# Splitting the last inverse-transform factor by even and odd frequency, on a quarter of the matrix engine each

## The chip, the cores and the metric

The kernel runs on one core of one Trainium2 chip. A core has a matrix engine (TensorE: PE in the profile, with its weight loads shown apart as PEld), a vector engine (DVE), a scalar engine (ACT), a general engine (POOL) and a queue engine (SP), which here only starts transfers (DMAs). The metric is the device time of the program in microseconds (us). Before the change the median of three runs is 2586.32 us (2583.95 to 2587.9).

## The reference

Two steps follow each other. The first is a filter in the frequency domain along the sequence; the second is a two-layer network with the ELU function between the layers. All is float32.

```python
# x: (8, 3008, 256); filt_r, filt_i: (1505, 256)
X = np.fft.rfft(x, axis=1)
y = np.fft.irfft(X * (filt_r + 1j * filt_i)[None], n=3008, axis=1)
# w_in: (256, 2048); w_out: (2048, 256)
h = y.reshape(24064, 256) @ w_in
out = np.where(h > 0, h, np.exp(np.minimum(h, 0)) - 1) @ w_out
```

## The kernel before, in words

**The transform.** The sequence of 3008 tokens is written as 47 x 64, so a token is 47·n2 + n1 with n2 from 0 to 63, and each direction of the transform takes two factors of matrix products with tables. Tokens n1 and 47 − n1 are handled as a pair i (24 pairs in all), because their tables are mirror images. The stages for one of the 8 batches b are: `x_unit` and `a_unit` (the first forward factor), `z_write` and `z_read` through memory, `b_unit` (the second forward factor), the products with the filter (`re_mult` to `im_sums`), `bi_unit` (the first inverse factor), `y_write`, and then, for each of six groups m of four pairs, `tn_read`, `y_read`, `n_unit` and `n_sums`. This last factor is what the diff touches.

`n_unit` sums over 128 rows, which are 32 frequencies k2 times four parts p (cosine and sine, of the pair's two sides). For each pair and each half dh of the 256 channels it multiplies a 128 x 128 tile of `t` (rows against channels) with a 128 x 128 tile of the table `tn` (rows against tokens: 64 values of n2 for n1, 64 for 47 − n1). That is eight matrix products a unit, into two PSUM banks, and ACT copies each bank to SBUF (`y0`, `y1`). The float32 product runs as two passes, so the profile shows 16 weight loads and 16 matmuls a unit.

**The network.** The two layers are computed with Strassen's scheme in Winograd's form: seven products in the place of eight, and sums ahead of them and behind them. Its blocks are the two channel halves and two token halves. `n_sums` makes the four sums of the input blocks on DVE (function `combine`: each a difference of two 128 x 256 tiles; 128 x 224 for m = 0, which has seven token sets in place of eight). `up_steps` makes the seven products of the first layer for a quarter q of the 2048 hidden columns, and the ELU: `keep` copies on ACT, `add` on DVE, `elu_exp` (two ACT instructions) and `elu_max` (one DVE instruction). `down_steps` makes the seven products of the second layer for the quarter before.

**The order.** It is written out by hand. One quad is one (b, m, q): seven U steps of this quarter and seven D steps of the one before, four matmul records each. A batch has 24 quads (`PER`). The transform's work is hung into the quads by a table, `at(quad, place, function)`: place 2 is behind the third step of the quad, place 3 behind the fifth, place 0 in the middle (behind seven or eight steps), place 1 behind the quad's last step and sums. Every engine runs its instructions in this order, so what is put at a place stands in line, on each engine that it uses, between the steps around it. With t the first quad of the batch before, the six units of `n_unit` stand at quads t+23, 25, 29, 32, 36, 40 and the network uses unit m from quad t+24+4m on. Their transfers are issued on SP's queue two quads earlier. The sums stand with the unit for m < 3 and one quad later, at place 1, for m > 2. A stage before the change that already uses parts of the matrix engine: `a_unit` has 64 x 64 tiles in groups of four (two row halves, two column halves), 256 columns wide; `b_unit` and `bi_unit` have sixteen tiles of 24 x 32.

The first batch has its own path (`a_first`, `t_first`, `b_first`, `bi_first`), since nothing else can run by then; weights are also prepared there on DVE and ACT, up to the fourth quad. `n_unit(0, 0)` and `n_sums(0, 0)` are called right ahead of the first quad.

In `up_steps` one DVE instruction will matter: step 7 puts its product into a bank "d", `add("b22", ...)` reads that bank, and step 4 then adds its own product into the same bank, so PE must not begin step 4 before that add has read it.

Of the kernel before, what the change touches and what calls it, by code (L numbers as in the profile page):

```python
# [26 lines left out]
P = 128  # L27
# [14 lines left out]
def _make_tables():  # L42
# [75 lines left out]
    gf = np.zeros_like(gb)  # L118
    for o in (0, 64):
        gf[o:o + 48] = gb[o:o + 48].reshape(2, H, 2, 64).swapaxes(0, 1).reshape(48, 2, 64)  # L120
    tn = np.ascontiguousarray(tn.reshape(4, K2, H, P).swapaxes(0, 1)).reshape(P, H, P)
    once = np.stack([np.eye(P), gf.reshape(P, P)], 1)
    return [t.astype(np.float32) for t in (ta, tn, np.stack([gb, gr, gi], 1), tf, once, pairs)]

# [7 lines left out]
def kernel(  # L132
# [60 lines left out]
    def bank(name, shape=(P, 2, D)):  # L193
        i = banks.pop(0)
        return i, psM.tile(list(shape), FP32, tag="m%d" % i, name=name)
# [271 lines left out]
                              t[32 * p:32 * p + 24])  # L467

    def tn_read(b, m):
        w = tns[b, m] = tnp.tile([P, 4, P], FP32, tag="tn", name="tn")  # L470
        nc.sync.dma_start(w, tn_d[:, 4 * m:4 * m + 4, :])

    def y_read(b, m, *parts):
        t = t4s[b, m] = t4p.tile([P, 4, D], FP32, tag="t4", name="t4")
        for k in parts or (slice(0, K2),):
            r = slice(4 * k.start, 4 * k.stop)
            nc.sync.dma_start(t[r], yds[b].rearrange("k (p i) d -> (k p) i d", p=4)[r, 4 * m:4 * m + 4, :])

    def half(m):

# [1 line left out]

    def n_unit(b, m):
        t, w, h = t4s.pop((b, m)), tns.pop((b, m)), half(m)
        rows = []
        for dh in range(2):
            y = yp.tile([P, 512], FP32, tag="y%d" % dh, name="y%d" % dh)
            k, ps = bank("psn", (P, 512))
            for q, i in enumerate(order(m)):
                nc.tensor.matmul(ps[:, ts(q, P)], t[:, i - 4 * m, ds(dh * P, P)], w[:, i - 4 * m, :],  # L490
                                 start=True, stop=True)
            nc.scalar.activation(out=y[:, 0:2 * h], in_=ps[:, 0:2 * h], func=AXT.Copy)
            banks.append(k)
            rows += [y[:, 0:h], y[:, h:2 * h]]
        s = yp.tile([P, 3, 256], FP32, tag="ys", name="ys")
        ys[b, m] = rows + [s[:, i, 0:h] for i in range(3)]

    def n_sums(b, m):
        ys[b, m] = combine(*ys[b, m])

    COMBO = {1: 0, 2: 2, 3: 6, 4: 3, 5: 4, 6: 5, 7: 1}

    def combine(b11, b12, b21, b22, t1, t2, t4):

        nc.vector.tensor_tensor(out=t1, in0=b12, in1=b11, op=ALU.subtract)
        nc.vector.tensor_tensor(out=b12, in0=b22, in1=b12, op=ALU.subtract)
        nc.vector.tensor_tensor(out=t2, in0=b22, in1=t1, op=ALU.subtract)
        nc.vector.tensor_tensor(out=t4, in0=b21, in1=t2, op=ALU.subtract)
        return {1: b11, 2: b21, 3: b22, 4: t4, 5: t1, 6: t2, 7: b12}  # L520

    G_TAGS = (("g1", ("b11", "b12")), ("g2", ("b21", "b22")), ("g3", ("t1", "t2")), ("g4", ("t4",)))
    UPS = (1, 2, 6, 5, 7, 3, 4)
# [2 lines left out]
    def up_steps(b, m, q):  # L526

        h = half(m)
        y = ys[b, m]
        g = {}  # L530
        for tag, names in G_TAGS:
            t = gp.tile([P, len(names), 2, 256], FP32, tag=tag, name=tag)
            g.update({n: t[:, i, :, 0:h] for i, n in enumerate(names)})
        held = {}

        def mm(n, key, start):
            if start:
                held[key] = bank("ph" + key)
            ps = held[key][1]
            for a in range(2):  # L540
                nc.tensor.matmul(ps[:, a, 0:h], w_in[q][:, COMBO[n], a, :], y[n],  # L541
                                 start=start and a == 0, stop=True, skip_group_check=True)
            return ps[:, :, 0:h]

        def done(key):
            banks.append(held.pop(key)[0])

        def add(o, i0, i1):
            nc.vector.tensor_tensor(out=g[o], in0=i0, in1=i1, op=ALU.add)  # L549

        def keep(o, i0):
            nc.scalar.activation(out=g[o], in_=i0, func=AXT.Copy)  # L552

        es = {}

        def elu_exp(n, src):
            e = es[n] = ep.tile([P, 2, 256], FP32, tag="e", name="e")[:, :, 0:h]
            nc.scalar.activation(out=e, in_=src, func=AXT.Relu, scale=-1.0)  # L558
            nc.scalar.activation(out=e, in_=e, func=AXT.Exp, scale=-1.0)  # L559

        def elu_max(n, src):

            nc.vector.scalar_tensor_tensor(out=g[n], in0=es[n], scalar=1.0, in1=src, op0=ALU.subtract, op1=ALU.max)  # L563


        def s1():
            keep("t1", mm(1, "s", True))

        def s2():
            add("b11", mm(2, "a", True), g["t1"])  # L570
            done("a")

        def s6():
            keep("t2", mm(6, "s", False))

        def s5():
            keep("t4", mm(5, "s", False))
            elu_exp("b11", g["b11"])

        def s7():  # L580
            add("b22", mm(7, "d", True), g["t4"])
            elu_max("b11", g["b11"])

        def s3():
            p = mm(3, "s", False)
            elu_exp("b12", p)
            elu_exp("b22", g["b22"])
            elu_max("b12", p)
            done("s")

        def s4():
            add("b21", mm(4, "d", False), g["t2"])
# [12 lines left out]

        return (s1, s2, s6, s5, s7, s3, s4), tail


# [47 lines left out]
    def o_unit(b, m):  # L656
# [3 lines left out]
        n = 7 if m == 0 else 8  # L660
        for k in range(2):
            nc.vector.transpose(out=o.rearrange("p (j k) e s -> p j k e s", k=2)[:, 0:n, k],
                                in_=c.rearrange("p e (j k s) -> p j k e s", k=2, s=32)[:, 0:n, k])

        o = o.rearrange("p (u f k) e s -> p u f k (e s)", u=4, f=2)
        queues = itertools.cycle((nc.sync, nc.scalar) if (b, m) == (B - 1, 5) else (nc.sync,))
# [114 lines left out]
    with tc.manual_schedule():  # L781
# [152 lines left out]
        for b in range(B):  # L934
            t = (b - 1) * PER
            if b > 0:
# [12 lines left out]
                for g in range(0, NG, 2):  # L949
# [13 lines left out]
                    at(s + 3, 2, im_sums, b, g)  # L963
                    at(s + 3, 1, bi_unit, b, g)
                    at(s + 3, 1, y_write, b, g)
            for m, (s, place) in enumerate(((23, 0), (25, 1), (29, 1), (32, 0), (36, 0), (40, 0))):
                if b > 0 or m > 0:
                    at(t + s - 2, 0, tn_read, b, m)
                    at(t + s - 2, 1 if m == 0 else 0, y_read, b, m)
                    at(t + s, place, n_unit, b, m)  # L970

                    at(*((t + s + 1, 1) if m > 2 else (t + s, place)), n_sums, b, m)
                if b == 0 and m == 1:
                    at(1, 1, w_join, 13)
                at(t + PER + 4 * m + 5, 0, c_unit, b, m)
# [58 lines left out]
```

## Time and profile before

| | |
|---|---|
| median of three runs | 2586.32 us |
| the profiled execution, own time | 2586.76 us |
| its span, first to last instruction | 2585.0 us |
| PE busy | 2543.5 us (98%), 14474 matmul records |
| DVE busy | 2040.2 us (79%) |
| ACT busy | 1550.4 us (60%) |
| DMA | 206 MB, 80 GB/s in the mean |
| `n_unit` matmuls (line 490) | 768 records, 93.6 us busy |

A line of the groups reads: source line, engine, operation, tile written and tiles read, shapes, number of instructions, then busy time in us and mean ns of one, then the engine's idle time just ahead of them and what ended it. A matmul's duration is a modelled one and overlaps the next; what a matmul costs PE is the distance from its start to the next one's. A timeline's line gives the start in us, the time from the first start to the last end of the merged instructions, the engine, the line, and their number.

### The profile page before, as it was taken

The numbers are of one execution on the slowest core, as the hardware profiler recorded it, in microseconds if no ns is written. First come the engines' busy times: TensorE is split into PE (matmuls) and PEld (weight loads), VectorE is DVE, ScalarE is ACT, GpSimd is POOL, SyncE is SP. The second block draws the span as 40 slices with busy tenths as digits, with TensorE's granted clock in tenths as the row PEclk, the third lists the DMA queues.
The fourth block names the chain that finished last, engine by engine and source line by source line (L and its number), as shares of the span: only waits on it lengthen the run. The fifth ranks groups of instructions, "written<-read, shape, count | busy, mean of one in ns | idle before, by whom it ended". The sixth has DMA issues, their size and how long they took to land.

```text
span 2585.0 us, 39447 instructions
## 1 busy us (share of the span) xinstructions
PE 2543.5 (98%) x14474; PEld 2199.1 (85%) x14474; DVE 2040.2 (79%) x3532; ACT 1550.4 (60%) x2715; POOL 159.7 (6%) x315
## 2 busy tenths in 40 slices
PE   5999999999999999999999999999999999999998
PEld 4788889888898888988889888888889888898887
DVE  6978887788878887688877888778886788866666
ACT  6766555655566555665565655565655655555554
POOL 5001000000000000000000000000100010000000
PEclk8999999999999999999999999999999999999999
DMA  9662223423233221523225231343213322110010
GB/s 280 184 185 70 58 49 81 131 62 73 51 103 96 71 69 41 135 74 81 49 54 142 69 78 37 78 124 84 67 41 85 90 62 65 39 48 20 22 29 17
DMA packets 229177, 206.35 MB, mean 80 GB/s; under 512 B 128666, under 2 KB 195418, under 8 KB 228984
## 3 DMA queue, kind: packets, MB, share of 16 engines
q1 hardware_dynamic: 213624, 172.94, 26.2%
q0 software_dynamic: 14000, 30.44, 4.3%
q8 instruction: 114, 1.87, 0.3%
q14 instruction: 79, 0.65, 0.1%
q10 hardware_dynamic: 1360, 0.46, 0.1%
HBM read 131.87 MB, written 78.17 MB: 81 GB/s over the span
## 4 chain that ended last, share of the span: by engine, by line
PE 96%; DMA 2%; DVE 1%; ACT 0%; issue 0%; SPq 0%; DVEq 0%; ACTq 0%
PE po L623 44%; PE phs L541 25%; PE phd L541 13%; PE pha L541 6%; PE psn L490 3%; PE psa L234 2%; PE pf L383 1%; PE pv L455 1%; DMA t<-in_moe_w_in_dram 1%; DMA wd<-in_moe_w_out_dram 1%; DMA xc<-in_x_dram 0%; DMA yd<-t 0%; PE po L330 0%; PE po L296 0%; PE psr L330 0%
## 5 line engine op out<-in xcount | busy, mean ns | idle before, releaser
L623 PE MATMUL po<-g,wo 128*128 128x256 f32 (+1 forms) x5376 | 1312.9, 376 | 0.0
L623 PEld LDWEIGHTS po<-g,wo 128*128 128x128 f32 x5376 | 1012.1, 190 | 163.2 <-issue 49.7
L552 ACT ACTIVATE g<-phs 128x512 f32<-128x512 f32 (+1 forms) x576 | 339.1, 589 | 747.6 <-PE phs L541 746.2
L559 ACT ACTIVATE e<-e 128x512 f32<-128x512 f32 (+1 forms) x768 | 477.2, 621 | 24.4
L549 DVE TENSOR_TENSOR g<-phd,g 128x512 f32<-128x512 f32 (+1 forms) x384 | 259.3, 675 | 289.6 <-ACT e L559 204.3
L541 PE MATMUL phs<-ys,wi 128*128 128x256 f32 (+1 forms) x1536 | 387.7, 375 | 1.5 <-ACT g L552 1.5
L541 PE MATMUL phs<-y,wi 128*128 128x256 f32 (+1 forms) x1536 | 387.7, 375 | 0.0
L563 DVE SCALAR_TENSOR_TENSOR g<-e,g 128x512 f32<-128x512 f32 (+1 forms) x576 | 386.8, 672 | 0.4 <-ACT e L559 0.2
L558 ACT ACTIVATE e<-g 128x512 f32<-128x512 f32 (+1 forms) x576 | 353.4, 614 | 44.7 <-DVE g L549 37.0
L541 PEld LDWEIGHTS phs<-ys,wi 128*128 128x128 f32 x1536 | 291.4, 190 | 35.4 <-ACT g L552 2.5
L541 PEld LDWEIGHTS phs<-y,wi 128*128 128x128 f32 x1536 | 287.6, 190 | 35.7 <-ACT g L552 0.2
L563 DVE SCALAR_TENSOR_TENSOR g<-e,phs 128x512 f32<-128x512 f32 (+1 forms) x192 | 129.8, 676 | 140.1 <-ACT e L559 139.7
L541 PE MATMUL phd<-ys,wi 128*128 128x256 f32 (+1 forms) x768 | 195.4, 377 | 2.3 <-DVE g L549 2.3
L541 PE MATMUL pha<-y,wi 128*128 128x256 f32 (+1 forms) x768 | 193.8, 375 | 0.0
L541 PE MATMUL phd<-y,wi 128*128 128x256 f32 (+1 forms) x768 | 193.7, 375 | 0.0
L558 ACT ACTIVATE e<-phs 128x512 f32<-128x512 f32 (+1 forms) x192 | 113.0, 589 | 128.9 <-PE phs L541 128.8
L541 PEld LDWEIGHTS phd<-ys,wi 128*128 128x128 f32 x768 | 144.4, 190 | 23.4 <-DVE g L549 7.7
L541 PEld LDWEIGHTS pha<-y,wi 128*128 128x128 f32 x768 | 145.2, 190 | 17.3
L541 PEld LDWEIGHTS phd<-y,wi 128*128 128x128 f32 x768 | 145.8, 190 | 16.5
L324 POOL DMA_DIRECT2D fall<-fp x224 | 110.0, 499 | 731.6 <-DVE r L428 704.5
L549 DVE TENSOR_TENSOR g<-pha,g 128x512 f32<-128x512 f32 (+1 forms) x192 | 129.0, 672 | 24.3 <-PE pha L541 24.3
L600 DVE TENSOR_TENSOR g<-g,g 128x512 f32<-128x512 f32 (+1 forms) x192 | 130.7, 681 | 6.7
(154 smaller groups left out, 2081.3 us busy)
## 6 DMA issues: line engine op xcount, KB each, us to landing
yd<-t SPq DMA_DIRECT2D x127, 192.0 KB
t<-yd SPq DMA_DIRECT2D x47, 512.0 KB
z<-t SPq DMA_DIRECT2D x84, 256.0 KB
fall<-fp POOLq DMA_DIRECT2D x224, 96.0 KB, 2.9
t<-z SPq DMA_DIRECT2D x224, 96.0 KB
out_dram<-o SPq DMA_DIRECT2D x632, 32.0 KB
tn<-tn_t SPq DMA_DIRECT2D x48, 256.0 KB
xc<-in_x_dram SPq DMA_DIRECT2D x84, 128.0 KB
```

Source lines behind the costliest of these rows:

```text
L234: nc.tensor.matmul(p[o:o + 64, u, :], w[r, u, o:o + 64], src[r, u, :], start=True, stop=True)
L324: nc.gpsimd.dma_start(t[32 * a:32 * a + 24].rearrange("p c u d -> p (c u d)"), fp[g, a].rearrange("q c u d -> q (c u d)"))
L383: nc.tensor.matmul(pf[p][1][32 * a:32 * a + 32, js, :], fb[r, v, :], t2[r, js, a, :], start=True, stop=True, tile_position=(32 * p, 32 * a))
L490: nc.tensor.matmul(ps[:, ts(q, P)], t[:, i - 4 * m, ds(dh * P, P)], w[:, i - 4 * m, :], start=True, stop=True)
L541: nc.tensor.matmul(ps[:, a, 0:h], w_in[q][:, COMBO[n], a, :], y[n], start=start and a == 0, stop=True, skip_group_check=True)
L549: nc.vector.tensor_tensor(out=g[o], in0=i0, in1=i1, op=ALU.add)
L552: nc.scalar.activation(out=g[o], in_=i0, func=AXT.Copy)
L558: nc.scalar.activation(out=e, in_=src, func=AXT.Relu, scale=-1.0)
L559: nc.scalar.activation(out=e, in_=e, func=AXT.Exp, scale=-1.0)
L563: nc.vector.scalar_tensor_tensor(out=g[n], in0=es[n], scalar=1.0, in1=src, op0=ALU.subtract, op1=ALU.max)
L600: nc.vector.tensor_tensor(out=b12, in0=b22, in1=b12, op=ALU.subtract)
L623: nc.tensor.matmul(po[i][:, u, 0:h], w_out[q][:, COMBO[n], a, :], g[n][:, a, :], start=q == 0 and a == 0 and n in (1, 3, 6, 4), stop=True, ...
```

## The change

The token 47·(n2 + 32) + n1 has, for even k2, the same table entry as 47·n2 + n1, and for odd k2 the negative one. So the sums over even and over odd k2 are made apart, for 32 values of n2 alone; the first token half is their sum and the second their difference.

- The table `tn` loses its second half of n2 (64 columns, not 128), its rows are sorted into 64 even and 64 odd ones, and the odd ones are scaled by −2. `tn_read` moves half the bytes. `y_read` is two DMAs, one for each parity of k2, in place of one.
- `n_unit` makes, for each pair, each channel half dh and each half c of its 128 channels, two products: one over the even rows, one over the odd. Each has 64 rows, 64 weight columns and 64 moving columns. The four of a (pair, dh) lie on four different 64 x 64 tiles of the array. There are 32 products a unit, 64 records. The even sums go to one bank, the odd ones to the other; both banks are taken at the unit's start. ACT copies each bank as before (two copies of 128 x 512).
- The token halves are now n2 below 32 and from 32 on. The odd sum scaled by −2 is itself one of Winograd's sums. `n_sums` makes the rest in five instructions: one scaled sum of 128 x 512 (`both` = even − 0.5·odd), one scaled sum and three differences of 128 x 256.
- Places: for m = 0 the sums' parts 0 to 2 stand with the unit and parts 3, 4 in the next quad at place 2; `n_unit` for m = 1 and 2 moves from place 1 to place 0 of its quad, with its last three sums at place 1; for m > 2 all sums move from place 1 of the next quad to place 2 of the quad after that.
- `elu_exp("b11")` moves from step 5 to step 7, behind what stands at place 0. The output's transposes read each token half as one stretch; their number and size stay.

```diff
-    tn = np.ascontiguousarray(tn.reshape(4, K2, H, P).swapaxes(0, 1)).reshape(P, H, P)
+    tn = tn.reshape(4, K2 // 2, 2, H, 2, 2, 32)[..., 0, :] * np.array([1.0, -2.0])[:, None, None, None]
+    tn = np.ascontiguousarray(tn.transpose(2, 1, 0, 3, 4, 5)).reshape(P, H, 64)
...
-        w = tns[b, m] = tnp.tile([P, 4, P], FP32, tag="tn", name="tn")
+        w = tnp.tile([P, 4, P], FP32, tag="tn", name="tn").rearrange("p a (q t) -> p (a q) t", t=64)[:, 0:4]
...
         for k in parts or (slice(0, K2),):
-            r = slice(4 * k.start, 4 * k.stop)
-            nc.sync.dma_start(t[r], yds[b].rearrange("k (p i) d -> (k p) i d", p=4)[r, 4 * m:4 * m + 4, :])
+            for r in range(2):
+                o = 64 * r
+                nc.sync.dma_start(t[o + 2 * k.start:o + 2 * k.stop].rearrange("q i d -> q (i d)"),
+                                  yds[b][k.start + r:k.stop:2].rearrange("k (p i) d -> k p (i d)", p=4)
+                                  [:, :, 4 * m * D:4 * m * D + 4 * D])
...
-        rows = []
-        for dh in range(2):
-            y = yp.tile([P, 512], FP32, tag="y%d" % dh, name="y%d" % dh)
-            k, ps = bank("psn", (P, 512))
-            for q, i in enumerate(order(m)):
-                nc.tensor.matmul(ps[:, ts(q, P)], t[:, i - 4 * m, ds(dh * P, P)], w[:, i - 4 * m, :],
-                                 start=True, stop=True)
-            nc.scalar.activation(out=y[:, 0:2 * h], in_=ps[:, 0:2 * h], func=AXT.Copy)
+        ps = [bank("psn", (P, 2, 256)) for _ in range(2)]
+        for q, i in enumerate(order(m)):
+            for dh in range(2):
+                for c in range(2):
+                    for (_, p), r in zip(ps, HALVES):
+                        nc.tensor.matmul(p[ts(c, 64), dh, ts(q, 64)], t[r, i - 4 * m, ds(dh * P + 64 * c, 64)],
+                                         w[r, i - 4 * m, :], start=True, stop=True)
...
+        for t, (k, p) in zip((even, odd), ps):
+            nc.scalar.activation(out=t, in_=p[:, :, 0:h], func=AXT.Copy)
             banks.append(k)
...
+        steps = ((both, odd, -0.5, even, ALU.add), (even[:, 1], odd[:, 1], 0.5, even[:, 1], ALU.add),
+                 (t2, even[:, 1], 1.0, odd[:, 0], ALU.subtract), (even[:, 0], t2, 1.0, both[:, 0], ALU.subtract),
+                 (odd[:, 1], both[:, 1], 1.0, t2, ALU.subtract))
+        for i in parts or range(5):
+            o, x, c, y, op = steps[i]
+            if c == 1.0:
+                nc.vector.tensor_tensor(out=o, in0=x, in1=y, op=op)
+            else:
+                nc.vector.scalar_tensor_tensor(out=o, in0=x, scalar=c, in1=y, op0=ALU.mult, op1=op)
...
-            elu_exp("b11", g["b11"])
-
         def s7():
+            elu_exp("b11", g["b11"])
             add("b22", mm(7, "d", True), g["t4"])
...
-            for m, (s, place) in enumerate(((23, 0), (25, 1), (29, 1), (32, 0), (36, 0), (40, 0))):
+            for m, s in enumerate((23, 25, 29, 32, 36, 40)):
...
-                    at(t + s, place, n_unit, b, m)
-                    at(*((t + s + 1, 1) if m > 2 else (t + s, place)), n_sums, b, m)
+                    if b == 0 and m == 1:
+                        at(t + s, 1, n_unit, b, m)
+                        at(t + s, 1, n_sums, b, m)
+                    else:
+                        at(t + s, 0, n_unit, b, m)
+                        for place, *parts in (((t + s, 0), 0, 1, 2), ((t + s + 1, 2), 3, 4)) if m == 0 else (
+                                ((t + s, 0), 0, 1), ((t + s, 1), 2, 3, 4)) if m < 3 else (((t + s + 2, 2),),):
+                            at(*place, n_sums, b, m, *parts)
```

More of the change, by code (lines that the diff above doesn't have):

```diff
@@ L469, in tn_read @@
     def tn_read(b, m):
-        w = tns[b, m] = tnp.tile([P, 4, P], FP32, tag="tn", name="tn")
+        w = tnp.tile([P, 4, P], FP32, tag="tn", name="tn").rearrange("p a (q t) -> p (a q) t", t=64)[:, 0:4]
+        tns[b, m] = w
         nc.sync.dma_start(w, tn_d[:, 4 * m:4 * m + 4, :])
@@ L484, in n_unit @@
         t, w, h = t4s.pop((b, m)), tns.pop((b, m)), half(m)
-        rows = []
-        for dh in range(2):
-            y = yp.tile([P, 512], FP32, tag="y%d" % dh, name="y%d" % dh)
-            k, ps = bank("psn", (P, 512))
-            for q, i in enumerate(order(m)):
-                nc.tensor.matmul(ps[:, ts(q, P)], t[:, i - 4 * m, ds(dh * P, P)], w[:, i - 4 * m, :],
-                                 start=True, stop=True)
-            nc.scalar.activation(out=y[:, 0:2 * h], in_=ps[:, 0:2 * h], func=AXT.Copy)
-            banks.append(k)
-            rows += [y[:, 0:h], y[:, h:2 * h]]
@@ L495, in n_unit @@
[L495 to L499, printed above, removed]
-    COMBO = {1: 0, 2: 2, 3: 6, 4: 3, 5: 4, 6: 5, 7: 1}
[L514 to L520, printed above, removed]
+        ps = [bank("psn", (P, 2, 256)) for _ in range(2)]
@@ new lines, in n_unit @@
+        for q, i in enumerate(order(m)):
[4 more added lines that the diff above has]
+                                         w[r, i - 4 * m, :], start=True, stop=True)
+        even, odd, both = (yp.tile([P, 2, 256], FP32, tag=n, name=n)[:, :, 0:h] for n in ("y0", "y1", "yb"))
+        t2 = yp.tile([P, 256], FP32, tag="yt", name="yt")[:, 0:h]
@@ new lines, in n_unit, with n_sums @@
+        ys[b, m] = {1: both[:, 0], 2: both[:, 1], 3: even[:, 1], 4: odd[:, 1], 5: odd[:, 0], 6: t2, 7: even[:, 0],
+                    "even": even, "odd": odd, "both": both}
+        for t, (k, p) in zip((even, odd), ps):
+            nc.scalar.activation(out=t, in_=p[:, :, 0:h], func=AXT.Copy)
+            banks.append(k)
+    def n_sums(b, m, *parts):
+        even, odd, both, t2 = (ys[b, m][k] for k in ("even", "odd", "both", 6))
+        steps = ((both, odd, -0.5, even, ALU.add), (even[:, 1], odd[:, 1], 0.5, even[:, 1], ALU.add),
[7 more added lines that the diff above has]
+                nc.vector.scalar_tensor_tensor(out=o, in0=x, scalar=c, in1=y, op0=ALU.mult, op1=op)
@@ L577, in s5, with s7 @@
             keep("t4", mm(5, "s", False))
+        def s7():
             elu_exp("b11", g["b11"])
-        def s7():
             add("b22", mm(7, "d", True), g["t4"])
@@ L662, in o_unit @@
             nc.vector.transpose(out=o.rearrange("p (j k) e s -> p j k e s", k=2)[:, 0:n, k],
-                                in_=c.rearrange("p e (j k s) -> p j k e s", k=2, s=32)[:, 0:n, k])
+                                in_=c[:, :, k * half(m):(k + 1) * half(m)].rearrange("p e (j s) -> p j e s", s=32))
         o = o.rearrange("p (u f k) e s -> p u f k (e s)", u=4, f=2)
```

## The prediction

> **What bounds the kernel now.** I read the page's busy row and its chain first, then stretches of the span.
>
> ```profile
> PE 2543.5 (98%) x14474; PEld 2199.1 (85%) x14474; DVE 2040.2 (79%) x3532; ACT 1550.4 (60%) x2715; POOL 159.7 (6%) x315
> ...
> PE 96%; DMA 2%; DVE 1%; ACT 0%; issue 0%; SPq 0%; DVEq 0%; ACTq 0%
> ```
> ```profile
> 88.00:104.00 16.00, 14.47 (x75) 12.93 (x74) 13.39 (x28) 11.91 (x22) 0.00 (x0) 1.00 0.88 223
> 104.00:136.00 32.00, 29.73 (x197) 27.44 (x199) 30.80 (x58) 22.99 (x40) 0.00 (x0) 1.00 0.47 130
> 136.00:2569.00 2433.00, 2433.00 (x13787) 2112.84 (x13779) 1924.62 (x3310) 1448.81 (x2536) 125.94 (x251) 1.00 0.28 72
> ```
>
> The stretches' columns are: the stretch, its length, busy us of PE, PEld, DVE, ACT, POOL, the granted clock, DMA share and GB/s. From 136 to 2569 us PE has no idle microsecond at full clock, while DVE is free for a fifth of the time. There, what shortens PE's stream shortens the span by as much, unless another engine turns late. Ahead of 136 us PE idles 3.8 us, and from 104 to 136 DVE is full (30.80 of 32): what is saved on PE there is not saved.
>
> Now one unit of the changed stage, from the timeline (start, time to the last end, engine, line):
>
> ```profile
> 1018.37 1.95 PE L490 MATMUL psn<-tn,t 128*128 128x128 f32 x16
> 1020.15 1.03 PE L623 MATMUL po<-g,wo 128*128 128x256 f32 x4
> 1020.25 0.96 ACT L492 ACTIVATE y<-psn 128x448 f32<-128x448 f32 x2
> 1021.02 1.03 PE L541 MATMUL phd<-y,wi 128*128 128x256 f32 x4
> 1022.34 0.68 DVE L549 TENSOR_TENSOR g<-phd,g 128x512 f32<-128x512 f32 x1
> 1023.61 1.03 PE L541 MATMUL phd<-ys,wi 128*128 128x256 f32 x4
> ```
>
> The unit holds PE from 1018.37 to 1020.15: 1.78 us, 111.3 ns a record at 128 columns. A record of 256 columns takes (1021.02 − 1020.15) / 4 = 216 ns.
>
> The shape the change wants, four tiles of 64 x 64, is there already in `a_unit`, line 234 (PE rows first, then two weight-load rows):
>
> ```profile
> 1036.67 1.03 PE L623 MATMUL po<-g,wo 128*128 128x256 f32 x4
> 1037.63 0.43 PE L234 MATMUL psa<-sd,ta 64*64 64x256 f32 x2
> 1037.64 0.43 PE L234 MATMUL psa<-xc,ta 64*64 64x256 f32 x2
> 1037.90 0.38 PE L234 MATMUL psa<-sd,ta 64*64 64x256 f32 x2
> 1037.91 0.38 PE L234 MATMUL psa<-xc,ta 64*64 64x256 f32 x2
> 1038.11 0.38 PE L234 MATMUL psa<-sd,ta 64*64 64x256 f32 x2
> ...
> 1039.20 0.38 PE L234 MATMUL psa<-xc,ta 64*64 64x256 f32 x2
> 1039.52 1.02 PE L623 MATMUL po<-g,wo 128*128 128x224 f32 x4
> 1040.38 0.54 PE L541 MATMUL phs<-y,wi 128*128 128x224 f32 x2
> ```
> ```profile
> 1037.63 0.14 PEld L234 LDWEIGHTS psa<-sd,ta 64*64 64x64 f32 x2 [0.33 <-issue]
> 1037.64 0.14 PEld L234 LDWEIGHTS psa<-xc,ta 64*64 64x64 f32 x2
> 1037.68 0.14 PEld L234 LDWEIGHTS psa<-sd,ta 64*64 64x64 f32 x2
> ```
>
> Four matmuls start within 0.02 us, and the next four 0.21 us later: four tiles run at once, each at the pace that a full matmul of 256 columns has. Their weight loads come in fours too, and a tile's second load starts 0.05 us behind its first.
>
> **Part 1: PE's work in a unit.** Removed: 16 records, 1.78 us. Added: 64 records in 16 groups of four, 64 moving columns and 64 weight columns, and two changes of tile shape.
>
> The changes' price is read from `a_unit`. The matmuls before it end their share at 1036.67 + 4 x 0.216 = 1037.53. The four of 224 columns behind it would take 4 x 0.189 = 0.756 and are done at 1040.38, so undisturbed they would have begun at 1039.62. Between are 2.09 us, of which 8 groups of 0.216 are 1.73: 0.36 us for going in and out.
>
> No row has a group with 64 columns. Bounds of its step: not under 0.054 us, a quarter of the 0.216 that a group of 256 columns takes, and not over 0.111 us, the step of the 128-column row, if halving the columns gained nothing. Nearest is the loads' row (0.05 us from one load to the next on a tile), and half of 0.1113 is 0.0557; with some nanoseconds of hand-over between load and matmul I take 0.0575. A unit is then 16 x 0.0575 + 0.36 = 1.28 us; saved 0.50 (bounds: 0.56 saved, 0.36 lost). Of 48 units the first two lie ahead of 136 us, so 46 x 0.50 = 23.0 us.
>
> The Trainium skill, "TensorE: Matmul & The Clock Gate", section "Wait — 56ns, not 53.3ns?", speaks against this: starts of two matmuls never come closer than about 25 ns, however few columns they have. By it a unit would be estimated at 64 x 25 ns + 0.36 = 1.96 us and the whole 8 us slower, before the start's cost. The rows above have four starts within 20 ns on different tiles, so I go by the rows; none shows more than 32 records in such a burst.
>
> **Part 2: the start.** Here PE waits for the transfer `t<-yd`, whose first matmul is at 86.55; the first U step follows at 88.45, as it needs `y0` alone (copy at 87.87, 0.52 us). After: 16 groups end at about 87.5; the copy of the even bank starts some 0.4 us later (as 87.87 stands to the first bank's last matmul at 87.40) and ends at 88.4, the odd one at 88.9; the first U step needs `both`, one DVE instruction of 448 elements (0.62 by line 549 at 90.34), so 89.5. Loss 1.05 us. `y_read` issues four DMAs for two, 0.43 to 0.5 us each on SP's queue at 81.80, the last of which PE waits for: between 0 and 1.0, I take 0.5. In the full DVE stretch the sums of unit (0, 1) cost 0.6 more (part 3): 0.5, as PE's own 0.5 there fills part of it. Together 2.1 us (bounds 1 to 4).
>
> **Part 3: DVE.** Removed: four instructions of 128 x 256 (0.42 us each, starting 0.40 apart). Added: one of 128 x 512 (0.61 apart by line 563) and four of 256: 0.61 us more a unit, 29 us in all. Cover: DVE's free 508 us between 136 and 2569. What counts is local: step 4 (PE row at 1023.61) waits for `add b22` (DVE at 1022.34, ends 1023.02), a margin of 0.6 us in a quad. If the sums ahead of it in DVE's line end late, PE stops.
> - m = 0, the quad shown: the copies now wait for the unit's end, 0.9 us after its start for the even bank; copies at about 1019.7 and 1020.2 (they no longer stand behind `elu_exp b11`), parts 0 to 2 from 1020.8 for 0.6 + 2 x 0.39 to 1022.1; step 7 ends at about 1021.4, `add b22` runs at 1022.1 to 1022.8, and step 4 is due 0.5 us earlier than before, at 1023.1. Fits by 0.3 us. Cost zero, bound 0.5 x 7.
> - m = 1, 2: only parts 0 and 1 stand ahead of `add b22`, less than for m = 0; zero. PE's work and ACT's two copies move half a quad forward; their transfer, issued two quads earlier (1017.50 for use near 1050), stays early.
> - m > 2: the sums leave the stretch behind one quad's tail and stand behind `add b11` in the next, ahead of two adds and the output's transposes. In such a quad DVE is idle for 2.95 us before `add b22` at 1164.89; the sums push the line back by about 1.8 us (0.6 longer, and starting only when step 2 is done). Zero.
>
> **Part 4: the rest.** ACT: same two copies; `elu_exp b11` comes at most 1.1 us later where copies stand ahead of it, and next quad's D steps need it 3 us and more later: zero. Both banks are taken at once: the second 0.9 us earlier than before, and it came free in the quad before: zero. SP: 46 more issues of 0.43 us; the tightest is the read for m = 0, issued 1008.84 and used at 1018.37; the second half would be issued near 1009.3 and landing took 4.4 us at the start: 4 us spare, zero. Its 16 output DMAs start 0.43 us later, which nothing on PE waits for. `tn` moves half: zero, as DMAs are busy 28%. Transposes: same size, zero. I add 0.4 us for small waits.
>
> **Sum.** 2586.76 (own time of the profiled execution) − 23.0 + 2.1 + 0.4 = 2566.3. The median of the three runs is 0.44 lower, so 2565.8.
>
> **Rivals.**
> 1. The groups don't keep the pace: the step stays at 0.111 us, because load and matmul of 64 columns on one tile don't overlap, or two tiles alone run at once. For it: no row has 64 moving columns under a fresh load. Against: loads in `a_unit` start beside running matmuls in fours. A unit would be 2.14 us, 0.36 more: 46 x 0.36 + 2.5 = 19 slower, 2605. It decides from a step of 0.089 us, where 16 steps and 0.36 make 1.78.
> 2. The same in part: a step of 0.073 us (between the two), as the second half of the 64 records arrives at PE's queue too late; the trace shows 32 in a burst at most. Unit 1.53, 46 x 0.25 − 2.5 = 9 saved: 2577.
> 3. DVE becomes late at `add b22`. If it had no cover, the 29 us would all appear: −23 + 29 + 2.5 = 8 slower, 2595. Against: 2.95 us idle in the quad for m > 2.
> 4. The change does what it says on PE, and as much appears as waits of PE for ACT's copies or DVE's sums in seven or more quads a batch: 2586. Against: waits for ACT are 4 us in the whole trace now.
>
> **How the numbers follow.** Forecast 0.73; rival 1 0.08; rival 2 0.12; rival 3 0.04; rival 4 0.03. By the forecast's bounds (a step of 0.054 and a start of 1 us, against 0.063 and 4 us) it lies between 2562 and 2573. Rival 2 reaches to 2580, so 2561 to 2580 leaves out rivals 1, 3, 4 and 3 in 100 of the rest. A change under 0.2% (5 us) can't be told from none. Faster: 0.73 + 0.12 = 0.85; within: rival 4 and a tail of rival 2, 0.04; slower: 0.11.
>
> **What the changed profile would show.** Line 490's successor with 3072 records, groups of four at 0.055 to 0.06 us, a unit of 1.25 to 1.3 us from its first matmul's predecessor to the next 128-wide one; PE still without idle time from 136 us on; first U step near 89.5 to 90; DVE some 29 us busier; `add b22` still ahead of step 4. Wrong would be: idle PE at line 541 `phd<-ys` behind DVE, or steps over 0.08 us.

## The result and the profile after

The changed kernel takes 2571.9 us (median of 4 runs, 2568.21 to 2572.39) against 2585.95 us for the kernel before (4 runs). The ratio is 0.9943, with a 95% interval from 0.9925 to 0.996: it is faster by 0.4 to 0.75%. The profiled execution's own time is 2571.72 us, 15.04 us less than that of before; the forecast for it was 20.5 less.

The page's busy row and its chain, of the kernel after:

```profile
PE 2525.8 (98%) x16778; PEld 2167.7 (84%) x16778; DVE 2069.0 (81%) x3580; ACT 1545.1 (60%) x2715; POOL 159.5 (6%) x315
...
PE 96%; DMA 2%; DVE 1%; issue 0%; SPq 0%; ACT 0%; DVEq 0%; ACTq 0%
```

PE still carries 96% of the chain. It has 2304 matmul records more and is busy for less time. DVE is busy 28.8 us more, which the chain doesn't show: its share is 1%, as before.

Now the stretches (stretch, length, busy us and instructions of PE, PEld, DVE, ACT and POOL, granted clock, DMA share, GB/s):

```profile
83.20:87.70 4.50, 0.45 (x4) 0.22 (x3) 3.48 (x8) 3.82 (x7) 0.00 (x0) 1.00 0.74 221
88.40:95.20 6.80, 4.98 (x41) 4.44 (x33) 2.87 (x7) 1.52 (x3) 0.00 (x0) 0.50 0.80 223
104.00:136.00 32.00, 29.18 (x232) 27.45 (x232) 30.47 (x59) 22.71 (x40) 0.00 (x0) 1.00 0.38 109
136.00:2554.00 2418.00, 2417.40 (x16026) 2082.71 (x16026) 1957.02 (x3364) 1447.23 (x2541) 125.92 (x251) 1.00 0.28 70
183.90:187.40 3.50, 3.50 (x31) 1.56 (x7) 0.86 (x2) 1.85 (x6) 0.00 (x0) 0.51 0.20 36
```

Two things are to be seen. From 136 us on PE still has no idle time to speak of (0.6 us of 2418). But it now has the granted clock at half in two places, 6.8 us from 88.4 and 3.4 us from 183.9, where the kernel before had full clock from 44.3 to 2580.4 us.

**Where the 15 us come from.** Both traces can be laid on each other by the first matmul of each quad (the first U step). The difference of the starts, after less before, in us:

| quad | 0 | 1 | 2 | 3 | 6 | 7 | 24 | 48 | 72 | 96 | 168 | 191 |
|---|---|---|---|---|---|---|---|---|---|---|---|---|
| after less before | +2.52 | +4.44 | +3.84 | +5.10 | +4.60 | +8.36 | +6.23 | +3.12 | +0.02 | −3.08 | −12.41 | −14.90 |

From quad 7 to the end the kernel gains 23.26 us, evenly: a batch of 24 quads takes 309.69 us in place of 312.79, 3.10 less. The six units are 6 x 0.50 of it; the rest is about 0.13 us in quad 21, where step 4 of the kernel before began late behind `add b22` and now doesn't. Against that stand 5.10 us lost up to quad 3 and 3.76 us lost between quads 6 and 7; one unit between quads 3 and 6 gives 0.5 back. 5.10 − 0.50 + 3.76 − 23.26 = −14.90. So the steady part did what was forecast, the start lost more than twice what was forecast, and the loss at quad 6 was not forecast at all.

**The steady part.** The timeline of the unit for m = 0 of a middle batch and of what follows it (start, time to the last end, engine, line, operation, tiles, number; in brackets the engine's idle time ahead and what ended it):

```profile
1018.03 1.02 PE L538 MATMUL phs<-y,wi 128*128 128x256 f32 x4
1018.98 1.16 PE L495 MATMUL psn<-tn,t 64*64 64x64 f32 x64
1020.07 1.13 PE L620 MATMUL po<-g,wo 128*128 128x256 f32 x4
1020.19 0.98 ACT L502 ACTIVATE y<-psn 128x448 f32<-128x448 f32 x2 [0.51 <-PE psn L495]
1021.20 0.62 DVE L515 SCALAR_TENSOR_TENSOR yb<-y,y 128x448 f32<-128x448 f32 x1 [3.71 <-ACT y L502]
1022.29 0.39 DVE L513 TENSOR_TENSOR yt<-y,y 128x224 f32<-128x224 f32 x1
1022.60 0.68 DVE L546 TENSOR_TENSOR g<-phd,g 128x512 f32<-128x512 f32 x1
1023.63 1.02 PE L538 MATMUL phd<-y,wi 128*128 128x256 f32 x4
```

The 64 records of line 495 start within 1.16 − 0.22 = 0.94 us of each other. Inside, four start within 0.02 us, and the next four 0.0585 us later (the first step of a burst alone takes 0.106). The share of the matmuls before them ends at 1018.03 + 4 x 0.216 = 1018.89; the next 128-wide ones, which would end undisturbed where they do, would have begun 1.288 us after that. All 47 units behind the first cost the same; before, a unit cost 1.786. The way in and out is 0.35 us (1.288 less 16 x 0.0585), as `a_unit` showed.

On DVE, `add b22` (line 546) runs at 1022.60 and ends at 1023.28; step 4, which waits for it, begins at 1023.63. The margin is 0.35 us. It is not the tightest one. In the quad two further on, where the unit for m = 1 stands, it is 0.21 us (1050.02 less 1049.19 + 0.62):

```profile
1049.19 0.62 DVE L546 TENSOR_TENSOR g<-phd,g 128x448 f32<-128x448 f32 x1
1050.02 0.92 PE L538 MATMUL phd<-y,wi 128*128 128x224 f32 x4
```

**The start.** The same view where the first unit runs:

```profile
81.35 3.32 SPq L480 DMA_DIRECT2D t<-yd  x4
86.59 0.30 PE L495 MATMUL psn<-tn,t 64*64 64x64 f32 x2 [3.24 <-issue]
87.70 1.46 PE L495 MATMUL psn<-tn,t 64*64 64x64 f32 x62 [0.81 <-DMA t<-yd]
89.22 0.98 ACT L502 ACTIVATE y<-psn 128x448 f32<-128x448 f32 x2 [2.14 <-PE psn L495]
90.29 0.62 DVE L515 SCALAR_TENSOR_TENSOR yb<-y,y 128x448 f32<-128x448 f32 x1 [3.54 <-issue]
90.97 1.86 PE L538 MATMUL phs<-yb,wi 128*128 128x224 f32 x4 [1.82 <-DVE yb L515]
```

The four reads take SP 3.32 us to issue, 0.63 to 0.97 us each, where the two of before took 0.99. PE begins with the rows of k2 that have landed and waits for the last ones until 87.70. From the first read's issue to there are 6.35 us, where they were 4.75 (81.80 to 86.55). From there to the first U step, which now waits for both copies and one DVE sum, are 3.27 us; they were 1.90. From the issue of the last row write to the first U step it is 13.16 us, and was 9.75; the program's first stages happened to be 0.9 us earlier in this execution, so quad 0 starts 2.52 later. It then takes 8.66 us in place of 6.74, with the clock at half.

**Quad 6.** PE's and SP's rows where batch 1's first unit of `b_unit` stands, after and then before:

```profile
177.10 3.83 SPq L315 DMA_DIRECT2D t<-z  x8
179.16 1.89 PE L620 MATMUL po<-g,wo 128*128 128x256 f32 x8
180.98 4.58 PE L384 MATMUL pf<-t,pairs 24*32 24x256 f32 x40
185.48 2.04 PE L620 MATMUL po<-g,wo 128*128 128x256 f32 x4
```
```profile
169.21 4.18 SPq L314 DMA_DIRECT2D t<-z  x8
176.38 1.72 PE L383 MATMUL pf<-t,pairs 24*32 24x256 f32 x40
178.03 1.13 PE L623 MATMUL po<-g,wo 128*128 128x256 f32 x4
```

The 40 matmuls that read what `t<-z` brings take 4.58 us instead of 1.72: they wait for rows that have not landed, though the view shows no idle time. The four matmuls behind them take 2.04 us in place of 1.13, with the clock at half. The eight reads were issued 7.9 us later than before, while PE was only 4.6 us later. The distance from the first read to the first matmul fell from 7.17 to 3.88 us. SP's queue had slipped by itself: from +5.1 us at batch 1's first z write to +7.9 at these reads. About 0.75 us of that is the second read issue of the unit for m = 2; most of the rest stands at loads of x whose issue took longer in this execution (1.30 and 1.58 us, where their neighbours take 0.43).

### The profile page after: what moved, and what is told of

Same layout as the page of the kernel before. It is cut to its first block, busy times and chain, and to the rows that moved or that the text cites. A ratio compares the mean times of both kernels' runs of the same rounds, so it can differ in the third digit from the quotient of the medians.

```text
span 2569.9 us, 44172 instructions
## 1 busy us (share of the span) xinstructions
PE 2525.8 (98%) x16778; PEld 2167.7 (84%) x16778; DVE 2069.0 (81%) x3580; ACT 1545.1 (60%) x2715; POOL 159.5 (6%) x315
## 4 chain that ended last, share of the span: by engine, by line
PE 96%; DMA 2%; DVE 1%; issue 0%; SPq 0%; ACT 0%; DVEq 0%; ACTq 0%
PE po L620 45%; PE phs L538 25%; PE phd L538 13%; PE pha L538 6%; PE psn L495 2%; PE pf L384 2%; PE psa L235 2%; PE pv L456 1%; DMA xc<-in_x_dram 1%; DMA x<-in_x_dram 0%; DMA yd<-t 0%; PE po L331 0%; PE po L297 0%; PE psr L331 0%; PE psa L278 0%
## 5 line engine op out<-in xcount | busy, mean ns | idle before, releaser
L538 PE MATMUL phd<-y,wi 128*128 128x256 f32 (+1 forms) x1536 | 388.6, 376 | 3.4 <-DVE g L546 3.4
L538 PEld LDWEIGHTS phd<-y,wi 128*128 128x128 f32 x1536 | 291.2, 190 | 39.3 <-DVE g L546 7.0
L538 PE MATMUL phs<-yb,wi 128*128 128x256 f32 (+1 forms) x768 | 194.9, 377 | 1.8 <-DVE yb L515 1.8
L538 PE MATMUL phs<-yt,wi 128*128 128x256 f32 (+1 forms) x768 | 194.4, 376 | 0.9 <-ACT g L549 0.9
L538 PE MATMUL pha<-yb,wi 128*128 128x256 f32 (+1 forms) x768 | 194.6, 376 | 0.0
L538 PEld LDWEIGHTS phs<-yb,wi 128*128 128x128 f32 x768 | 144.0, 191 | 21.2 <-DVE yb L515 2.0
L538 PEld LDWEIGHTS phs<-yt,wi 128*128 128x128 f32 x768 | 146.6, 191 | 17.6 <-ACT g L549 1.2
L538 PEld LDWEIGHTS pha<-yb,wi 128*128 128x128 f32 x768 | 146.2, 191 | 17.0 <-ACT fall L393 0.2
```

## Experiments

My theory after this was: the PE term and DVE's cover are as forecast; the rest is three losses near the start, namely (a) the reads' issue and PE's idle time behind it, (b) the half clock that the idle time brings, (c) the reads of z that SP issues late. The rivals: that four small matmuls in place of one have another cause of gain than running side by side; that the moved sums aren't needed; and that the second DMA as such is the cost at the start.

**Do the four tiles run at once?** The kernel after with the loops turned, so that neighbours stay on one tile for eight products:

```diff
-        for q, i in enumerate(order(m)):
-            for dh in range(2):
-                for c in range(2):
-                    for (_, p), r in zip(ps, HALVES):
+        for c in range(2):
+            for (_, p), r in zip(ps, HALVES):
+                for q, i in enumerate(order(m)):
+                    for dh in range(2):
```

> The changed kernel with the same 32 products a unit in another order: all eight of one tile, then all of the next, so that no two neighbours lie on different tiles. Theory: the gain comes from four tiles at once; a record then takes 0.058 us by itself, 64 of them 3.7 us, a unit with its changes of shape 4.0 us in place of 1.29, and the kernel is 47 x 2.7 = 127 us slower than the changed one, near 2700. Rival: the unit is short because the products are half as many, and the order is of no account (the array finds the free tile by itself, as its queue looks ahead): near 2572.

Measured: 2675.0 us (one run). The unit takes 3.53 us, from this line of the timeline and its neighbours:

```profile
1054.98 3.40 PE L495 MATMUL psn<-tn,t 64*64 64x64 f32 x64
```

On one tile the records stand 0.058 us apart, the same step that a group of four has in the changed kernel. 64 of them would take 3.7; they take 3.18 from first to last, since neighbours overlap where the tile changes. A batch is 13.46 us longer than in the changed kernel, six times 3.53 − 1.288; the whole is 103 us longer. Here, 0.058 us is what one tile needs for a record of 64 moving columns with a fresh load, and the gain comes from four tiles at once. Without that the change would lose 89 us against the kernel before.

**Are the moves of the sums part of the gain?** All five sums back at the old places in one piece, and `elu_exp b11` back in step 5:

```diff
             keep("t4", mm(5, "s", False))
+            elu_exp("b11", g["b11"])
 
         def s7():
-            elu_exp("b11", g["b11"])
             add("b22", mm(7, "d", True), g["t4"])
...
-                        for place, *parts in (((t + s, 0), 0, 1, 2), ((t + s + 1, 2), 3, 4)) if m == 0 else (
-                                ((t + s, 0), 0, 1), ((t + s, 1), 2, 3, 4)) if m < 3 else (((t + s + 2, 2),),):
-                            at(*place, n_sums, b, m, *parts)
+                        at(*((t + s + 1, 1) if m > 2 else (t + s, 0)), n_sums, b, m)
```

> The changed kernel with the sums all in one piece at their places of before (with the unit for m below 3, one quad later at place 1 for m above 2), and the first exponential of a quad back ahead of place 0. Theory: the moves are what keeps the vector engine's new wait (its first sum needs both banks' copies) off the matrix engine: without them the add that step 4 needs ends 1.1 us late in the quads of m = 0 and 1.4 us late in those of m = 1 and 2: 7 x 1.1 + 15 x 1.4 = 29 us slower than the changed kernel, idle time of the matrix engine at phd behind the vector engine. Rival: the vector engine has cover everywhere: no difference.

Measured: 2600.58 us (one run), 28.7 above the changed kernel and some 15 above the kernel before. A batch takes 313.93 us, 4.24 more than with the moves: 1.61 in the quad of m = 1, 1.40 in that of m = 2, 1.10 in that of m = 0, and 0.13 in quad 21. The quads of m > 2 lose nothing, so their move isn't what the gain rests on. The stretch and the quad of m = 1 in this kernel's timeline:

```profile
136.00:2580.00 2444.00, 2419.12 (x16014) 2073.23 (x16013) 1954.72 (x3361) 1446.78 (x2538) 126.06 (x251) 1.00 0.28 70
```
```profile
1057.43 0.69 DVE L515 SCALAR_TENSOR_TENSOR yb<-y,y 128x512 f32<-128x512 f32 x1 [4.92 <-ACT y L502]
1059.42 0.42 DVE L513 TENSOR_TENSOR y<-yb,yt 128x256 f32<-128x256 f32 x1
1059.76 0.62 DVE L546 TENSOR_TENSOR g<-phd,g 128x448 f32<-128x448 f32 x1
1060.43 0.68 PEld L538 LDWEIGHTS phd<-y,wi 128*128 128x128 f32 x4 [1.69 <-DVE g L546]
1060.43 1.02 PE L538 MATMUL phd<-y,wi 128*128 128x224 f32 x4 [1.34 <-DVE g L546]
```

PE is idle for 24.9 us between 136 and 2580. All five sums stand ahead of `add b22` and start only when ACT's copies are done (1057.43), so the add ends at 1060.38, and step 4 begins right then, after 1.34 us of idle time. That is the third rival, DVE late at `add b22`, made real: DVE does the same work in both kernels, and only its place in the line differs. The forecast gave it 29 us without cover; that figure was DVE's added work, and the 28.7 measured are PE's waits, so that they agree is partly chance. The run moved the sums and `elu_exp` back together and doesn't divide the loss between them.

**The clock at the start.** The program has seven warm matmuls ahead of the first unit that do nothing but keep PE busy; four more of them:

```diff
-            for k in range(7):
+            for k in range(11):
```

> The changed kernel with eleven matmuls that only keep the matrix engine busy ahead of the first unit, in place of seven (their last ends near 86.8 us, not 83.4). Theory: of the changed kernel's loss of 5.1 us up to quad 3, some 2 us come from the clock at half from 88.4 to 95.2 us, which the kernel before did not have, and it came because the matrix engine idled from 83.4 to 87.7. Then the clock stays full from 44 us on, quad 0 takes 6.7 us and not 8.7, and the time is 1 to 2 us shorter, 2570 to 2571, or more if the late read at quad 6 is caught too. Rival: the loss at the start is all dependency (unit, copies, sum), and the clock, full or half, changes nothing that matters: within 0.5 us of 2571.9.

Measured: 2567.77 us (2567.27 to 2574.2), ratio to before 0.9928 [0.9908, 0.9947]; the changed kernel stood at 2571.9. The stretch of this kernel that had half clock in the kernel after:

```profile
88.40:95.20 6.80, 4.34 (x41) 3.63 (x33) 4.78 (x12) 2.32 (x5) 0.00 (x0) 1.00 0.96 207
```

The clock is full, and quad 0 takes 6.74 us, exactly what it took before the change, in place of 8.66. So 1.92 us of the start's loss are the clock. By time alone the run shows less: its ratio's interval overlaps that of the changed kernel, and 2 us of this profile's gain stand at quad 6, where it lost 1.7 us (quads 6 to 8) and not 3.76.

What put the clock at half? PE was busy for all of 83.2 to 87.7 here, where the changed kernel was busy for 0.45 of 4.50 us. But the length of one wait doesn't decide it. The traces show more. In each of the 13 traces all changes of the clock stand at whole multiples of 3.413 us from each other. So one can cut a trace into windows of that length on this grid and read PE's busy time in each. The windows at the start in the kernel after (the first line), in the kernel before (the next two) and in the kernel with eleven warm matmuls and later loads, which is described below (the last):

```profile
84.96:88.37 3.41, 0.97 (x47) 0.89 (x51) 1.75 (x4) 2.09 (x4) 0.00 (x0) 1.00 0.94 276
81.83:85.25 3.42, 1.87 (x5) 0.56 (x3) 3.34 (x8) 3.35 (x6) 0.00 (x0) 1.00 0.73 179
85.25:88.66 3.41, 2.11 (x17) 2.07 (x18) 2.00 (x5) 3.17 (x7) 0.00 (x0) 1.00 0.97 322
86.61:90.02 3.41, 1.23 (x63) 1.12 (x63) 0.72 (x2) 0.98 (x2) 0.00 (x0) 1.00 0.96 265
```

The first and the last are followed by half clock, the other two are not. In the kernel before PE was idle for 2.85 us in one piece, but the end of a window fell into it. In the last, no wait was longer than 1.83 us, but that one fell whole into the window, with the end of the wait before it. Over all windows of the 13 traces that begin at full clock, those with 1.46 us of busy PE or less are followed by half clock and those with 1.50 us or more are not. The two exceptions stand at quad 6, where the profile counts matmuls that wait for their rows as busy. So in these traces the clock goes to half when PE is busy for less than some 43% of a window, and where the windows fall differs from execution to execution. The Trainium skill, "TensorE: Matmul & The Clock Gate", Part 1, says that an idle window of about 3.4 us, counted by a window that runs on its own, puts the clock at half. The grid here agrees with that; the windows here were not idle, but busy for up to 1.46 us.

**Is it the second DMA as such?** The kernel before, with each read split in two halves of the partitions, in its own simple form:

```diff
-            nc.sync.dma_start(t[r], yds[b].rearrange("k (p i) d -> (k p) i d", p=4)[r, 4 * m:4 * m + 4, :])
+            for e in range(2):
+                r = slice(4 * k.start + 2 * (k.stop - k.start) * e, 4 * k.start + 2 * (k.stop - k.start) * (e + 1))
+                nc.sync.dma_start(t[r], yds[b].rearrange("k (p i) d -> (k p) i d", p=4)[r, 4 * m:4 * m + 4, :])
```

> The kernel before the change with each read of the third factor's rows in two transfers of 64 partitions in place of one of 128. Theory: this part of the change costs at the start: the first unit begins 0.5 to 1.1 us later, and SP's queue is about 0.9 us later at quad 6; in all 1 to 2 us slower, up to 5 if the late read at quad 6 or the half clock comes with it. Rival: two shorter transfers land no later than one long one, and SP has room: no change.

Measured: 2585.77 us (10 runs), ratio 0.9997 [0.9988, 1.0007]: nothing. So the second DMA as such costs nothing in the whole time. From the last row write's issue to the first U step it is 9.78 us (9.75 before), but this agreement is not the reads' own: the first matmul of the unit comes 6.57 us after that write (7.85 before), and the U step then waits for ACT, which still prepares weights. In the steady part the halves take SP 0.45 and 0.59 us to issue, where the changed kernel's two reads take 0.52 and 0.59 and the one read of before 0.43; so there the form of the read makes next to no difference. Only at the start do they differ: the changed kernel's four reads, which pick every second k2, take 0.63 to 0.97 us each, those of the simple form 0.26 to 0.56. That this form is what costs at the start fits these numbers, but no run changed the form alone.

**The reads of z at quad 6.** Two kernels aim at SP's queue. The first moves the DMAs of `f_pairs`, which stand in SP's line ahead of these reads, to POOL's queue; it was also run together with the eleven warm matmuls.

```diff
-        nc.sync.dma_start(dst[:, :, 0, :], src[:, 0:48:2, :])
+        nc.gpsimd.dma_start(dst[:, :, 0, :], src[:, 0:48:2, :])
...
```

> The changed kernel with the filter's rearrangement in the first five quads (16 transfers of up to 384 KB) issued on POOL's queue in place of SP's. Theory: the 3.75 us lost between quads 6 and 7 come from SP's queue, which by then runs 7.9 us later than before the change while the quads run 4.6 later, so that the first second-factor unit waits for its rows; with these issues gone from SP that wait (4.6 us for 40 records, where 1.85 is undisturbed) and the half clock at 184 to 187 us vanish: quad 7 minus quad 6 is 14.8 us as before the change and the time 3 to 4 us shorter, 2568 to 2569. Rival: the rows are late because their writer (the matrix engine and ACT) is late, whatever the queue: no change.

> Both: eleven warming matmuls, and the filter's rearrangement off SP's queue. Theory: the gains add, about 5 us: 2566 to 2568, and what remains of the start's loss is about 3 us. Rival: they are the same loss seen twice, and together give what the better of them gives alone.

Measured: 2572.77 us (ratio 0.994 [0.9923, 0.9958]) and 2574.32 us (0.9944 [0.9925, 0.9963]), no better than the changed kernel. The loss at quad 6 is gone in both (quads 6 and 7 start 8.56 us later than before in the first). But quad 0 starts at 94.92 in the first, and the half clock lasts from 85.5 to 99.2. On POOL's queue eleven of the fourteen transfers are issued between 63.5 and 82.6 us, where SP issued them from 105 us on; the row writes `yd<-t` that the first unit needs then take 7.4 us to land in place of 4.3. The edit removed one loss and made another of the same size. For the question it doesn't decide: the reads of z went out 4.8 us earlier, but PE also came to them 4 us later.

The second kernel moves the loads of x of batch 2 behind these reads:

```diff
-                                at(t + s, 1, x_load, nb, nxt)
+                                at(t + s + (6 if b == 1 and nb == 2 else 0), 1, x_load, nb, nxt)
```

> The changed kernel with the loads of batch 2's first four input chunks (24 transfers), which stand on SP's queue ahead of the reads for batch 1's first second-factor unit, issued six quads later. Nothing is added to the start this time. Theory: the loss between quads 6 and 7 comes from the line on SP's queue: its reads are issued some 10 us earlier, quad 7 begins 14.8 us after quad 6 as before the change, and the time is up to 3.7 us shorter, 2568 to 2570, with the start's loss left as it was. Rival: the rows are late because those who write them are late: quad 6 keeps its loss.

Measured: 2567.54 us (2565.27 to 2568.94), ratio 0.9932 [0.9917, 0.9947]. SP's and PE's rows of this kernel:

```profile
160.85 3.40 SPq L315 DMA_DIRECT2D t<-z  x8
178.32 1.72 PE L384 MATMUL pf<-t,pairs 24*32 24x256 f32 x40
179.98 1.13 PE L620 MATMUL po<-g,wo 128*128 128x256 f32 x4
```

The reads go out 17 us ahead of their use, the 40 matmuls take their 1.72 us, and quads 6 and 7 both start 1.95 us later than before the change: no loss there. So it was SP's line, as the distance of 3.88 us had suggested. The 13 traces agree on it: where the first read goes out 6.03 us or more ahead of the first matmul, the 40 matmuls take 1.72 us; at 4.52, 4.30, 3.88 and 2.51 us they take 2.83, 3.12, 4.58 and 5.79. That the median fell by 4.4 us isn't this alone (and here too the interval overlaps that of the changed kernel): in this execution the start lost 2.44 us up to quad 3 and not 5.10, with an unchanged start.

**How steady are the losses?** The changed kernel again, unedited, and on the same chip the two repairs (eleven warm matmuls, later loads) together:

> The changed kernel itself, so that the two below are compared with it on one chip. 2572, and in its profile a start's loss of 5 us up to quad 3 and a loss at quad 6 that comes and goes between 0 and 4 us.

> Eleven warming matmuls and batch 2's first input loads six quads later, without the third edit (the first unit's odd rows on POOL's queue). Theory: the two edits cure two different losses, the half clock of the start (2 us in quad 0) and the line at quad 6 (up to 3.8 us), so they add: 2565 to 2567. Rival: with the start 2 us earlier the line at quad 6 has moved as well, so that one of the two is enough: 2567 to 2568, like each alone.

Measured: 2572.36 us (2569.58 to 2574.29), ratio 0.994 [0.9927, 0.9954], and 2568.12 us (2564.98 to 2569.63), ratio 0.9927 [0.9915, 0.994]. In this profile of the unedited kernel quads 6 to 8 lose 6.6 us, not 3.75, and the clock is at half in three stretches, one of them between 122.4 and 125.8. So the losses differ from one execution to the next. The start differs too. Four profiles have the same program up to quad 0: the changed kernel, this second run of it, the kernel with later loads, and the one with the sums at their old places. Quad 0 begins at 90.97, 89.68, 88.19 and 90.93 us in them, and the loss up to quad 3 is 5.10, 5.45, 2.44 and 5.17 us. From the last row write's issue to quad 0 they lie nearer together: 12.66 to 14.04 us, against 9.75 and 9.78 in the two kernels without the change. With both repairs the loss at quad 6 is gone, but the clock at the start was at half for 3.4 us from 90.0 even so, and quad 0 took 8.28 us. The two repairs together are no better in the median than each alone; why they don't add, beyond the start's own spread, the runs don't settle.

**Both repairs and a third edit.** The third issues the first unit's reads of odd k2 on POOL's queue beside SP's; the kernel was run on two chips:

```diff
-                nc.sync.dma_start(t[o + 2 * k.start:o + 2 * k.stop].rearrange("q i d -> q (i d)"),
+                queue = nc.gpsimd if parts and r else nc.sync
+                queue.dma_start(t[o + 2 * k.start:o + 2 * k.stop].rearrange("q i d -> q (i d)"),
```

> The changed kernel with three edits at the start alone: eleven warming matmuls in place of seven; batch 2's first input loads six quads later; and, for the very first unit, the odd half of the rows read through POOL's queue while SP issues the even half. Theory: the start's loss falls from 5.1 us to some 2 us (the clock stays full, the last rows land about 1 us earlier) and quad 6 loses nothing: 2564 to 2567, faster than the changed kernel by 5 to 8 us. Rival: POOL's queue starts its transfers later than SP's, so the third edit takes back what the first gives: 2567 to 2569.

> The two edits and the third, again: 2564 to 2566. Theory: the third edit is worth what the last rows land earlier, about 1 us against the two edits alone. Rival: it is worth nothing, and the two edits alone reach the same.

Measured: 2564.84 us (2563.69 to 2565.96), ratio 0.992 [0.9908, 0.9932], and 2565.78 us (2564.54 to 2566.47), ratio 0.9919 [0.9906, 0.9933]. The second stood beside the unedited kernel on the same chip and was 6.6 us faster. SP's two reads of the first unit take 1.80 us to issue, POOL's two beside them 0.57 to 0.59 each, and in the first run's profile quad 0 starts at 89.43 and takes 6.74 us. Against the two repairs alone it is 2.3 us in the medians, with intervals of the ratios that overlap. So this last step is likely but not shown.

## Why the prediction was right and where it wasn't

The time, 2571.9, lies in the range, 6 us above the forecast. The direction and its cause were right; two terms of the sum were wrong. That the time still lies within the forecast's own bounds (2562 to 2573) is in part luck: the upper bound allowed for a slower step in the units and a start of 4 us, and what used it up was a start of 5.1 us and a wait that the sum had at zero. By the time alone rival 2 (2577) was as near as the forecast (2565.8); the profile tells them apart.

- **Part 1, PE's work in a unit: right.** Step 0.0585 us (forecast 0.0575), in and out 0.35 (0.36), unit 1.288 (1.28), saved 0.50, over 46 units 22.9 us (forecast 23.0). The 23.26 us from quad 7 on have 45 units; some 0.9 us of them is the wait in quad 21, which wasn't forecast. `a_unit`'s rows, 256 columns wide, were a good guide to 64 columns, and the loads' distance of 0.05 us was the nearest row to the step. Rivals 1 and 2 are out: no step over 0.06 us but the first of a burst (0.106, part of the way in, as the 0.27 us to the second group in `a_unit`'s rows), and 64 records in a burst keep the pace.
- Against the skill's figure the rows were the better guide. By the floor of 25 ns from start to start ("TensorE: Matmul & The Clock Gate", "Wait — 56ns, not 53.3ns?") the unit was estimated at 1.96 us; here 64 starts lie in 0.94 us, 15 ns apart in the mean, on four tiles.
- **Part 3, DVE: right.** 28.8 us busier (29 forecast), none of it on the path from quad 7 on; for m = 0, 0.35 us of margin at step 4 (0.3 forecast). The order was wrong: for m = 1 the prediction expected more room than for m = 0, and there are 0.21 us. Rivals 3 and 4 are out for this kernel, and the run with the sums at their old places shows what rival 3's mechanism is worth when the cover is gone: 28.7 us.
- **Part 2, the start: mis-sized, 2.1 forecast, 5.1 measured** (the bounds ended at 4), and the first U step at 90.97, not 89.5 to 90. Three of its terms can be compared, in this one execution. The dependency on both copies and a sum was 1.05, and is 1.37 (3.27 less 1.90; in the run with eleven warm matmuls, at full clock, it is 3.16 less 1.90, so a tenth of it is clock). The reads were 0.5, priced by the old form's 0.43 to 0.5 us an issue; they are 1.6 (6.35 less 4.75), and the new reads issue in 0.63 to 0.97 us each. The sums in the full DVE stretch were 0.5, and are 0.66 (quad 1 to quad 3). What was missing is the clock: the forecast let PE wait longer and didn't ask what the longer wait does to the clock afterwards. That is 1.92 us in quad 0. Another 0.44 us lies between the last row write and the first read, and the earlier first stages give 0.89 back: 1.37 + 1.6 + 0.66 + 1.92 + 0.44 − 0.89 = 5.10.
- **Part 4, "SP: zero": wrong by 3.76 us.** The step failed in its choice of place. (An added issue was also priced at 0.43 us and is 0.68 in the steady part, 0.52 + 0.59 less 0.43; there it costs nothing.) I took the tightest read in the steady part (the one for m = 0) and found 4 us spare, which held: PE has no idle time there. But SP's line is also late near the start, where it works through the loads that the first stages left behind. The reads of z for batch 1 had 7.17 us from issue to use, came 3.3 us closer, and PE stood; the last part of the loss, 2.04 in place of 1.13 us, is the clock at half behind it.

## What to carry to other kernels

Where a product can be cut into pieces of 64 rows and 64 weight columns, four tiles do four pieces in the time of one, if neighbours in the instruction stream lie on different tiles; the price is the way in and out of the shape (0.35 us here) and what the sums then cost elsewhere. Price a changed DMA by its own form and not by the form that it replaces, and follow its queue to the place where it is already late, not only to the steady part. Where a change makes PE wait longer once, ask how much of each window of 3.4 us it is still busy, and not only how long one wait is: here a wait that grew by about a microsecond cost twice that in clock.

## What was not expected of the hardware

- A record of 64 moving columns with a fresh 64 x 64 load costs 0.058 us on its tile whether or not three other tiles run beside it.
- PE idle for 2.85 us in one piece kept the full clock, and a wait of 1.83 us that fell whole into one window of 3.413 us, with the end of another, did not. In all 13 traces the busy time of such a window decides (1.46 us or less: half clock; 1.50 or more: full), but for the two at quad 6.
- Matmuls that wait for their operands, which the profile shows as busy, were followed by half clock too (at quad 6, for 3.4 us in the kernel after and 6.8 us in its second run).
- At the start, a read that picks every second k2 took SP 0.63 to 0.97 us to issue, against 0.26 to 0.56 for plain halves; in the steady part there was no such difference (0.52 to 0.59 against 0.45 to 0.59).
- In the version with three repairs the clock was at half once more, for 3.4 us from 121.8 us, where the changed kernel's first profile had none: the stretches at half move between executions and kernels in the first 200 us, and single profiles there are to be read with that in mind.
